# Linear attention and two feed-forward layers on one core: load order of the first pairs, order of the xh and xl pieces, place of the quotient steps and of layer two's weight conversions, queue of the x2 loads

## The chip, the cores and the metric

The kernel runs on one core of a Trainium2 chip. The metric is the device time of one execution in microseconds (us); lower is better. The engines are PE (matrix products), DVE (vector), ACT (scalar, with its activation functions), POOL (GpSimd) and SP (SyncE, which here issues almost all DMA transfers). Each engine works through its own instructions in order. A DMA issue stands in the stream of the engine that issues it, so an issue that waits holds up what is behind it.

## The reference

```python
# q, k, v: (4 batches, 8 heads, 576 tokens, 64); w_phi: (64, 128)
def phi(x):
    proj = np.einsum('bhsd,df->bhsf', x, w_phi)
    proj = proj - np.max(np.abs(proj), axis=-1, keepdims=True)
    return np.concatenate([np.exp(proj), np.exp(-proj)], axis=-1)
q_p, k_p = phi(q), phi(k)
kv = np.einsum('bhsf,bhsd->bhfd', k_p, v)
z = np.sum(k_p, axis=2)
num = np.einsum('bhsf,bhfd->bhsd', q_p, kv)
den = np.einsum('bhsf,bhf->bhs', q_p, z)[..., None] + 1e-06
x = (num / den).transpose(0, 2, 1, 3).reshape(2304, 512)
h = x @ w_in;   x2  = np.maximum(0.01 * h, h) @ w_out        # layer one: 512 -> 2048 -> 512
h = x2 @ w_in2; out = (h / (1 + np.exp(-h))) @ w_out2        # layer two: 512 -> 2048 -> 512
```

The weights of both layers reach the kernel as 64-bit words. The kernel turns them into 32-bit floats itself ("conversion").

## The kernel before

**Numbers in two pieces.** Most products are made from a high piece and a low piece of each operand: an ACT copy writes the rounded high piece, and DVE subtracts it from the value for the low one (`sub`, L262). Three products (high by high, high by low, low by high) replace one. Names ending in `h` and `l` are such pairs: `xh`/`xl`, `gh`/`gl`, `KVH`/`KVL`, `qh`/`ql`.

**Attention.** Work is in 16 pairs of heads, `(b, hp)`. Pairs 0 to 7 run first, in plain 32-bit (functions `f_...`): products of `k` (`f_pk` L418, `f_kt` L423/L429), of `q` (`f_pq` L453), a maximum over partitions on POOL (`f_pr` L475), exponentials on ACT (L301/L302, L493/L494), the sum over tokens (`kv_sign` L382/L387), its copy `KV` (`f_kc` L503), the quotient's products (`f_n` L516), their division (`f_nd` L532 to L534) and the writing of x (`f_fx`, through `put_x`). Pairs 8 to 15 run in high and low pieces (`s_...`): split of `k` and `q` (`s_split` L271, L279), the products of `k` (`s_pk`, L315 to L317), products of `q` (`s_pq` L347/L348, p copies L350, POOL maximum L352), `s_eq` (L362, L369, L370), the sum `s_kv` (L387, then `KVH` L400 on ACT and `KVL` on DVE), the numerator and denominator (`num_split`, L568, L571, L572), and `s_fin`. `num_split` sends the denominator through four DMAs: `e<-d`, then a reciprocal on DVE, `rec<-e`, `d<-rec`, all issued by SP. `s_fin` (fin0 and fin1 for the two halves of a pair) multiplies `x` by `d` (L588, DVE) and calls `put_x`, which for each token tile that the half touches makes `xh` (L408, ACT) and `xl` (DVE).

**Layer one.** 2304 tokens are five tiles of 462 or 460 (`tiles1`), and d_ff is 16 blocks of 128. A slot is one tile and one block: `h_mm` (12 products, L830), `h_g` (leaky relu into `g`, L836, ACT), `h_high` (`gh`, L841, ACT), `h_low` (`gl`, DVE), then `y_mm` (12 products, L861), one slot later in program order. A pair of the second half of the attention spans three slots, and the x of a tile is written about half a tile before the tile begins. After a tile, `y_out` stores it to `x2` in DRAM.

**Layer two.** `prep_x2` loads groups of 768 tokens from `x2` (`b1` L804, `b2` L805), forms four combinations of them on DVE (L808 to L811) and splits them. The layer is a seven-product scheme over 2 by 2 blocks. Its weights are prepared by `prep_w7` in units: load (L650), conversion on ACT (`narrow_act` L657, L658) and DVE (L664 to L670), sums (L717 to L720), split into `wst`, store to `w7s` (L713). `load_hl` loads them back as `ws` (L898); L942 and L1019 are the products. `raw` has 3 buffers (shared by weight words and `b1`/`b2`), `wst` 3 (shared with layer one's `wo` copies).

**What sets the order.** `ORDER`, `PLAN`, `SLOTS` and `EARLY` are hand-written times, sorted into one list `seq`; `run_att` takes steps from it and emits them. For engines in `pins` (PE, ACT, DVE), `in_order` notes the instructions of a step with its time, and `pin` chains those with a time under 150 in that order, without semaphores. All else is ordered by a scheduler that takes the program's order as priority and hoists what can run earlier. `behind(first, f)` emits `f` and ties each of its instructions behind the instruction in `first` of the same engine. `gate` is such a `first`: it holds layer two's conversions (`run_jobs`, `settle`) behind the split of pair 13's `k`. In `ORDER`, `flq` and `flv` are the loads of q/k and of v of pairs 0 to 7, all issued on SP; `va`, a pair's v, has 128 x 10 x 65 floats, 325 KB.

Of the kernel before, what the change touches and what calls it, by code (L numbers as in the profile page):

```python
# [18 lines left out]
    flq=(-0.1, 0.1, 0.4, 12.4, 23.9, 35.4, 46.9, 58.4),  # L19
    fpq0=(6.75, 10.01, 20.52, 27.8, 39.22, 50.72, 62.21, 73.71),  # L20
    fpq1=(7.22, 10.48, 20.99, 28.27, 39.69, 51.19, 62.68, 74.18),
    fpk=(4.47, 7.94, 21.45, 28.74, 40.16, 51.66, 63.15, 74.65),
# [12 lines left out]
    fqx0=(11.61, 19.16, 32.22, 44.23, 55.73, 67.22, 78.7, 89.4),  # L35
    flv=(0.0, 0.9, 22.9, 34.4, 45.9, 57.4, 68.9, 80.4),
    fqx1=(13.88, 22.28, 34.3, 45.8, 57.29, 68.79, 80.21, 91.65),
# [84 lines left out]
def tile_linear_attention_ffn_ffn(ctx: ExitStack, tc: tile.TileContext, q, k, v, w_phi, w_in1, w_out1, w_in2, w_out2, out):  # L122
# [48 lines left out]

    pins = {mybir.EngineType.PE: [], mybir.EngineType.Activation: [], mybir.EngineType.DVE: []}

# [9 lines left out]

    gate = {}

# [81 lines left out]
    def s_split(i):  # L267

        st = P[i]
        h, l = at([128, S0], F32R, "krh"), at([128, S0], F32R, "krl")  # L270
        a = nc.scalar.activation(h, st["kr"], AF.Copy)  # L271
        b = sub(l, st["kr"], h)
        if i == 13:
            gate.update({x.ins.engine: x.ins for x in (a, b)})
        st["krh"], st["krl"] = h, l
        qs = at([128, 2, S], F32R, "qs")
        for j in range(2):
            r, o = (slice(0, 64), slice(64, 128))[:: 1 - 2 * j]
            nc.scalar.activation(qs[r, j], st["qr"][r], AF.Copy)  # L279
            sub(qs[o, j], st["qr"][r], qs[r, j])  # L280
        st["qs"] = qs
        t = at([128, 128], F32R, "kth")
        nc.scalar.activation(t, st["kt"], AF.Copy)
        sub(t[64:128], st["kt"][64:128], t[64:128])
        st["kth"] = t
# [106 lines left out]
    def s_kv(i):  # L392
        st = P[i]
        for s in (1, 0):
            pv = kv_sign(i, s)
        h, l = st["KVH"], st["KVL"] = at([128, 2, 2, 2, D], F32R, "KVH"), at([128, 2, 2, 2, D], F32R, "KVL")
        for j in range(2):
            kv_, z_ = pv[:, :, j, 0:D], pv[:, :, j, D : D + 1].to_broadcast([128, 2, D])
            for slot, sr in ((j, kv_), (1 - j, z_)):
                nc.scalar.activation(h[:, j, :, slot, :], sr, AF.Copy)  # L400
                sub(l[:, j, :, slot, :], sr, h[:, j, :, slot, :])

    def put_x(i, rows, src, t0, n):

        b, hp = i // HP, i % HP
        for t, o, s0, n in segments(b * S + t0, n):
            xh, xl = x1_tile(t)
            nc.scalar.activation(xh[rows, hp, o : o + n], src[:, s0 : s0 + n], AF.Copy)  # L408
            sub(xl[rows, hp, o : o + n], src[:, s0 : s0 + n], xh[rows, hp, o : o + n])

# [219 lines left out]
    def run_att(until, tile_=None):  # L630
        while seq and (seq[-1][0] < until or (tile_ is not None and missing(tile_))):
# [8 lines left out]
            else:  # L640
                fns[n_](i)

# [151 lines left out]
    def prep_x2(u):  # L794
# [6 lines left out]
        for kk in range(2):  # L801
            b1 = wp.tile([128, 2, NB], F32, tag="raw", bufs=RAWB, name="b1")
            b2 = wp.tile([128, 2, NB], F32, tag="raw", bufs=RAWB, name="b2")
            nc.sync.dma_start(b1, x2[kk, :, a : a + 2 * NB].rearrange("p (j n) -> p j n", j=2))  # L804
            nc.sync.dma_start(b2, x2[kk + 2, :, a : a + 2 * NB].rearrange("p (j n) -> p j n", j=2))  # L805
            t1, t3 = (wp.tile([128, NB], F32, tag="t64", bufs=2, name="t1") for _ in range(2))
# [32 lines left out]
    def h_high(t, c):  # L839
        gh = G[t, c]["h"] = gp.tile([128, tiles1[t][1]], F32R, tag="gh", name="gh", bufs=2)  # L840
        nc.scalar.activation(gh, G[t, c]["g"], AF.Copy)  # L841

    def h_low(t, c):
        gl = G[t, c]["l"] = gp.tile([128, tiles1[t][1]], F32R, tag="gl", name="gl", bufs=2)
        sub(gl, G[t, c]["g"], G[t, c]["h"])

# [358 lines left out]
```

## Time and profile before

| what | value |
|---|---|
| median of 3 runs | 950.11 us (949.8 to 950.48) |
| profiled execution | 950.13 us |
| span of its instructions | 948.3 us, so 1.83 us lie around it |
| instructions | 15702 |

The span runs from the first to the last instruction that the profiler saw. What lies around it is in the time of an execution too. An engine that is idle costs time only where the work that ends last had to wait for it.

### The profile page before, as it was taken

Reading aid. Unit: us, or ns where it says so; the run is one execution under the profiler, and the core shown is the slowest. Engines: PE = TensorE matmul, PEld = TensorE weight load, DVE = VectorE, ACT = ScalarE, POOL = GpSimd, SP = SyncE. Lnnn points to the kernel's source line nnn. Section 1 sums busy time; section 2 is a strip of 40 time slices with the busy share of each in tenths; the row PEclk is TensorE's granted clock in tenths of the full one; section 3 lists DMA queues with packets and bytes.
Section 4 is the critical chain, followed back from the end, with each engine's and each line's share of the span. In section 5 each row is a group of like instructions: output and inputs, shape, how many; then the busy total and the mean of one; then the engine's idle time right before and its main releaser. Section 6 shows DMA issues by size and latency. Waiting matters only on the chain.

```text
span 948.3 us, 15702 instructions
## 1 busy us (share of the span) xinstructions
PE 937.1 (99%) x5430; PEld 883.5 (93%) x5430; DVE 649.2 (68%) x1280; ACT 596.3 (63%) x1224; POOL 70.6 (7%) x38
## 2 busy tenths in 40 slices
PE   8999999999999999999999999999999999999998
PEld 7999989999988989888888899999999999999998
DVE  6889999966676753478777667779653695534853
ACT  6888787877786765456655555566544565444553
POOL 3343000210112110000000000000000000000000
PEclk9999999999999999999999999999999999999999
DMA  9921474473343322599999988997898778986785
GB/s 339 373 76 59 135 253 152 175 228 105 119 143 110 118 101 66 196 354 366 366 335 343 408 309 285 337 335 277 273 299 278 238 241 264 305 272 222 249 265 171
DMA packets 102528, 226.14 MB, mean 238 GB/s; under 512 B 15024, under 2 KB 25264, under 8 KB 102448
## 3 DMA queue, kind: packets, MB, share of 16 engines
q1 hardware_dynamic: 102160, 224.86, 69.9%
q8 instruction: 44, 0.72, 0.3%
q14 instruction: 36, 0.29, 0.1%
q10 hardware_dynamic: 288, 0.26, 0.1%
HBM read 177.82 MB, written 47.22 MB: 237 GB/s over the span
## 4 chain that ended last, share of the span: by engine, by line
PE 84%; DMA 9%; ACT 4%; DVE 1%; SPq 1%; issue 1%; DVEq 0%; ACTq 0%
PE ps_y L1019 19%; PE ps_y L861 17%; PE ps_a L830 17%; PE ps_a L942 10%; PE ps_y L942 8%; PE ps_a L387 3%; DMA d<-rec 3%; DMA rec<-e 2%; PE ps_a L516 2%; PE ps_y L387 2%; DMA e<-d 1%; PE ps_y L516 1%; DMA w7s<-wst 1%; PE ps_a L568 1%; DMA ws<-w7s 1%
## 5 line engine op out<-in xcount | busy, mean ns | idle before, releaser
L830 PE MATMUL ps_a<-xh,wi 128*128 128x460 f32 (+1 forms) x640 | 196.3, 373 | 1.7 <-ACT g L836 1.6
L1019 PE MATMUL ps_y<-gt,ws 128*128 128x384 f32 x1008 | 177.5, 337 | 0.0
L1019 PEld LDWEIGHTS ps_y<-gt,ws 128*128 128x128 f32 x1008 | 176.4, 188 | 0.4 <-DMA ws<-w7s 0.4
L861 PE MATMUL ps_y<-gh,wo 128*128 128x460 f32 (+1 forms) x640 | 149.5, 372 | 1.1 <-ACT gh L841 1.1
L830 PEld LDWEIGHTS ps_a<-xh,wi 128*128 128x128 f32 x640 | 120.2, 188 | 16.3 <-ACT g L836 2.6
L861 PEld LDWEIGHTS ps_y<-gh,wo 128*128 128x128 f32 x640 | 119.2, 188 | 15.3 <-ACT gh L841 2.2
L830 PE MATMUL ps_a<-xl,wi 128*128 128x460 f32 (+1 forms) x320 | 118.8, 371 | 0.0
L942 PE MATMUL ps_a<-xs,ws 128*128 128x384 f32 x546 | 104.4, 338 | 0.5 <-DMA ws<-w7s 0.5
L942 PEld LDWEIGHTS ps_a<-xs,ws 128*128 128x128 f32 x546 | 96.7, 188 | 1.2 <-DMA ws<-w7s 0.8
L684 ACT ACTIVATE gt<-g 128x384 fp32r<-128x384 f32 x120 | 62.9, 525 | 53.3 <-PE ps_y L1019 51.8
L262 DVE TENSOR_TENSOR gt<-g,gt 128x384 fp32r<-128x384 f32 x120 | 66.3, 555 | 34.4 <-ACT gt L684 33.8
L942 PE MATMUL ps_y<-xs,ws 128*128 128x384 f32 x462 | 88.2, 338 | 0.4 <-DVE g L917 0.4
L942 PEld LDWEIGHTS ps_y<-xs,ws 128*128 128x128 f32 x462 | 81.7, 188 | 0.9 <-DVE g L917 0.7
L861 PE MATMUL ps_y<-gl,wo 128*128 128x460 f32 (+1 forms) x320 | 82.4, 373 | 0.0
L262 DVE TENSOR_TENSOR gl<-g,gh 128x460 fp32r<-128x460 f32 (+1 forms) x80 | 50.8, 635 | 25.5 <-ACT gh L841 16.0
L861 PEld LDWEIGHTS ps_y<-gl,wo 128*128 128x128 f32 x320 | 60.0, 188 | 6.9
L830 PEld LDWEIGHTS ps_a<-xl,wi 128*128 128x128 f32 x320 | 60.3, 188 | 6.0
L836 ACT ACTIVATE g<-ps_a 128x460 f32<-128x460 f32 (+1 forms) x80 | 44.0, 550 | 25.3 <-PE ps_a L830 24.6
L841 ACT ACTIVATE gh<-g 128x460 fp32r<-128x460 f32 (+1 forms) x80 | 46.7, 585 | 11.4 <-PE ps_y L861 10.2
L352 POOL PARTITION_ALL_REDUCE m<-p x16 | 35.3, 2208 | 236.1 <-ACT p L350 193.1
L387 PE MATMUL ps_a<-va,ke 128*128 128x128 f32 x384 | 46.9, 275 | 0.0
L934 ACT ACTIVATE g<-g 128x384 f32<-128x384 f32 x72 | 37.3, 520 | 14.8 <-DVE g L917 14.6
(168 smaller groups left out, 1501.0 us busy)
## 6 DMA issues: line engine op xcount, KB each, us to landing
ws<-w7s SPq DMA_DIRECT2D x336, 256.0 KB, 4.1
wo<-wos SPq DMA_DIRECT2D x64, 512.0 KB, 5.2
w7s<-wst SPq DMA_DIRECT2D x48, 512.0 KB, 6.2
raw<-in_moe_w_out_dram SPq DMA_DIRECT2D x32, 512.0 KB, 5.7
rawi<-in_moe_w_in_dram SPq DMA_DIRECT2D x16, 512.0 KB, 8.7
wos<-wo SPq DMA_DIRECT2D x16, 512.0 KB, 2.9
raw<-in_moe_w_in_dram SPq DMA_DIRECT2D x16, 512.0 KB, 6.7
va<-in_v_dram SPq DMA_DIRECT2D x16, 325.0 KB, 4.4
```

The costliest lines, as they stand in the source:

```text
L262: return nc.vector.tensor_tensor(out_, x, h.bitcast(F32), op=ALU.subtract)
L352: nc.gpsimd.partition_all_reduce(m, p, 128, bass_isa.ReduceOp.absmax)
L387: nc.tensor.matmul(pv[:, s, j], ke[:, g, s, :], vf[:, w : w + NKV], start=False, stop=(j == 1 and c == 3), skip_group_check=True)
L516: nc.tensor.matmul(pb[:, w : w + NNUM], e[:, s, cs], KV[:, s, j], start=(s == 0), stop=(s == 1))
L684: nc.scalar.activation(h, f, AF.Copy)
L830: nc.tensor.matmul(ph, a[:, kk, :], b_[:, kk, :], start=(m == 0), stop=(m == 3 * KD - 1))
L836: nc.scalar.activation(g, G[t, c]["ph"], AF.Prelu, alpha=0.01)
L841: nc.scalar.activation(gh, G[t, c]["g"], AF.Copy)
L861: nc.tensor.matmul(Y[t][d][:, 0:n], a[:, ds_], b_, start=(c == 0 and m == 0), stop=(c == NC - 1 and m == 1), skip_group_check=True)
L934: nc.scalar.activation(g[j], x, AF.Silu)
L942: nc.tensor.matmul(bank[b_], w[:, a, kk], x[:, c, kk], start=(first and m == 0), stop=(m == 5), skip_group_check=True)
L1019: nc.tensor.matmul(bank[b_][db], w[:, a, db], t[:, c], start=(first and p == 0 and m == 0), stop=(p == NP - 1 and m == 2), skip_group_chec ...
```

## The change

1. `ORDER`: the q products of pair 2 (`fpq0[2]`, `fpq1[2]`) move from 20.52/20.99 to 15.9/16.0, and the load of v of pair 0 (`flv[0]`) from 0.0 to 0.2, behind the q/k loads of pair 1.
2. `pins` also has SP, so DMA issues of steps that are emitted through `in_order` with a time under 150 (q/k/v loads, layer-one weight loads, stores of `wos`) are chained in the written order.
3. `put_x` makes all `xh` copies first, and then all `xl`.
4. `gate` is set by the last `KVH`/`KVL` of the last pair in place of the split of pair 13.
5. `low` holds the latest `gh` (ACT) and `gl` (DVE) emitted so far; fin0 and fin1 of pairs 8 to 15 are tied behind them.
6. The twelve loads of `x2` (384 KB each) are issued by GpSimd in place of SP.

```diff
-    fpq0=(6.75, 10.01, 20.52, 27.8, 39.22, 50.72, 62.21, 73.71),
-    fpq1=(7.22, 10.48, 20.99, 28.27, 39.69, 51.19, 62.68, 74.18),
+    fpq0=(6.75, 10.01, 15.9, 27.8, 39.22, 50.72, 62.21, 73.71),
+    fpq1=(7.22, 10.48, 16.0, 28.27, 39.69, 51.19, 62.68, 74.18),
...
-    flv=(0.0, 0.9, 22.9, 34.4, 45.9, 57.4, 68.9, 80.4),
+    flv=(0.2, 0.9, 22.9, 34.4, 45.9, 57.4, 68.9, 80.4),
...
-    pins = {mybir.EngineType.PE: [], mybir.EngineType.Activation: [], mybir.EngineType.DVE: []}
+    pins = {mybir.EngineType.PE: [], mybir.EngineType.Activation: [], mybir.EngineType.DVE: [], mybir.EngineType.SP: []}
...
-    gate = {}
+    gate, low = {}, {}
...
-        a = nc.scalar.activation(h, st["kr"], AF.Copy)
-        b = sub(l, st["kr"], h)
-        if i == 13:
-            gate.update({x.ins.engine: x.ins for x in (a, b)})
+        nc.scalar.activation(h, st["kr"], AF.Copy)
+        sub(l, st["kr"], h)
...
-                nc.scalar.activation(h[:, j, :, slot, :], sr, AF.Copy)
-                sub(l[:, j, :, slot, :], sr, h[:, j, :, slot, :])
+                ops = nc.scalar.activation(h[:, j, :, slot, :], sr, AF.Copy), sub(l[:, j, :, slot, :], sr, h[:, j, :, slot, :])
+        if i == B * HP - 1:
+            gate.update({x.ins.engine: x.ins for x in ops})
...
-        for t, o, s0, n in segments(b * S + t0, n):
-            xh, xl = x1_tile(t)
-            nc.scalar.activation(xh[rows, hp, o : o + n], src[:, s0 : s0 + n], AF.Copy)
-            sub(xl[rows, hp, o : o + n], src[:, s0 : s0 + n], xh[rows, hp, o : o + n])
+        parts = [(*[x[rows, hp, o : o + m] for x in x1_tile(t)], src[:, s0 : s0 + m]) for t, o, s0, m in segments(b * S + t0, n)]
+        for xh, xl, x in parts:
+            nc.scalar.activation(xh, x, AF.Copy)
+        for xh, xl, x in parts:
+            sub(xl, x, xh)
...
-                fns[n_](i)
+                behind(low if n_[:3] == "fin" else {}, fns[n_], i)
...
-            nc.sync.dma_start(b1, x2[kk, :, a : a + 2 * NB].rearrange("p (j n) -> p j n", j=2))
-            nc.sync.dma_start(b2, x2[kk + 2, :, a : a + 2 * NB].rearrange("p (j n) -> p j n", j=2))
+            nc.gpsimd.dma_start(b1, x2[kk, :, a : a + 2 * NB].rearrange("p (j n) -> p j n", j=2))
+            nc.gpsimd.dma_start(b2, x2[kk + 2, :, a : a + 2 * NB].rearrange("p (j n) -> p j n", j=2))
...
-        nc.scalar.activation(gh, G[t, c]["g"], AF.Copy)
+        low[mybir.EngineType.Activation] = nc.scalar.activation(gh, G[t, c]["g"], AF.Copy).ins
...
-        sub(gl, G[t, c]["g"], G[t, c]["h"])
+        low[mybir.EngineType.DVE] = sub(gl, G[t, c]["g"], G[t, c]["h"]).ins
```

## Rows read from the trace of the kernel before

**Rows 1.** The page: span, and busy us (share) of the engines.
```profile
span 948.3 us, 15702 instructions
...
PE 937.1 (99%) x5430; PEld 883.5 (93%) x5430; DVE 649.2 (68%) x1280; ACT 596.3 (63%) x1224; POOL 70.6 (7%) x38
```

**Rows 2.** Windows: busy us (x instructions) of each engine, granted clock, DMA share, GB/s.
```profile
0.00:20.00 20.00, 17.16 (x102) 14.52 (x103) 11.89 (x19) 13.41 (x30) 8.85 (x10) 1.00 0.91 327
...
260.00:280.00 20.00, 19.19 (x113) 17.55 (x112) 15.47 (x30) 15.26 (x35) 4.28 (x2) 1.00 0.51 165
...
380.00:400.00 20.00, 19.38 (x94) 17.16 (x93) 8.64 (x18) 9.53 (x19) 0.00 (x0) 1.00 0.51 165
...
640.00:660.00 20.00, 19.51 (x111) 19.05 (x110) 18.85 (x39) 12.20 (x27) 0.00 (x0) 1.00 0.72 260
760.00:780.00 20.00, 19.59 (x112) 19.27 (x111) 18.73 (x39) 12.82 (x28) 0.00 (x0) 1.00 0.77 239
```

**Rows 3.** Waits of PE in 219 to 366: sum in us, times, longest.
```profile
PE ps_a L830 <- ACT g L836: 1.6, 4, 0.8
PE ps_a L568 <- DVE KVL L262: 0.5, 1, 0.5
```

**Rows 4.** Chain that ended last, 219 to 262: start, us, what.
```profile
226.75 2.81 PE ps_a L830 x12
...
234.08 1.78 PE ps_a L387 x16
...
236.60 2.53 PE ps_a L830 x12
```

**Rows 5.** Timeline of the start: start, us, engine, line, out<-in, [idle before <-releaser].
```profile
8.99 1.10 PE L418 MATMUL ps_y<-wc,kr 128*128 128x256 f32 x4 [0.98 <-DMA kr<-in_k_dram]
...
10.19 1.94 DVE L483 TENSOR_TENSOR m<-p,m 128x512 f32<-128x512 f32 x1 [0.79 <-POOL m L475]
...
15.63 0.72 ACT L494 ACTIVATE qh<-m 128x640 f32<-128x640 f32 x1
...
16.15 0.68 DVE L483 TENSOR_TENSOR m<-p,m 128x512 f32<-128x512 f32 x1
...
16.59 0.60 ACT L503 ACTIVATE KV<-ps_y 128x512 f32<-128x512 f32 x1 [0.24 <-PE ps_y L387]
...
17.25 2.05 PE L516 MATMUL ps_y<-KV,qh 128*128 128x128 f32 x16 [0.69 <-ACT KV L503]
...
31.14 0.27 ACT L408 ACTIVATE xh<-ps_a 128x114 fp32r<-128x114 f32 x1 [1.37 <-DVE xl L262]
...
31.73 0.19 PEld L516 LDWEIGHTS ps_a<-KV,qh 128*128 128x128 f32 x1 [0.26 <-ACT p L464]
```

**Rows 6.** Timeline, attention beside layer one, and the first slots after it.
```profile
237.91 0.45 ACT L408 ACTIVATE xh<-x 128x288 fp32r<-128x288 f32 x1 [2.98 <-DVE x L588]
...
238.26 0.26 ACT L400 ACTIVATE KVH<-ps_a 128x128 fp32r<-128x128 f32 x1
...
268.73 0.66 ACT L657 ACTIVATE t<-raw 128x512 f32<-128x512 f32 x1
...
391.02 0.45 ACT L408 ACTIVATE xh<-x 128x288 fp32r<-128x288 f32 x1 [4.86 <-DVE x L588]
...
392.58 1.72 PE L861 MATMUL ps_y<-gh,wo 128*128 128x460 f32 x7 [0.62 <-ACT gh L841]
...
403.37 0.90 PE L861 MATMUL ps_y<-gh,wo 128*128 128x460 f32 x3 [0.51 <-ACT gh L841]
```

**Rows 7.** SP's queue in layer two: one row of its waits, then the timeline.
```profile
SPq L804 <- DVE t L810: 8.5, 1, 8.5
...
620.19 0.95 SPq L713 DMA_DIRECT2D w7s<-wst  x1
...
645.36 8.83 SPq L898 DMA_DIRECT2D ws<-w7s  x14
...
650.98 1.33 PE L942 MATMUL ps_a<-xs,ws 128*128 128x384 f32 x6 [0.49 <-DMA ws<-w7s]
```

## The prediction

> **What bounds the kernel now.** I read the page first. The span is 948.3 us and PE, the matmul engine, is busy for 937.1 of it [rows 1]; every window shows a granted clock of 1.00 [rows 2]. So nothing in this change can pay unless it closes a gap on PE: DVE, ACT and POOL are busy for 649.2, less and less again, and their idle time costs nothing by itself. The page leaves about 11 us of gaps. The windows say where some of them are: of 20 us PE misses 2.84 at the start, 0.81 in 260 to 280, 0.49 in 640 to 660, 0.41 in 760 to 780 [rows 2]. The waits of PE over 219 to 366 us, where full attention work runs beside layer one, name the releasers: four waits of L830 (layer one's first product) on `g` of L836, 1.6 us, longest 0.8, and one of L568 on `KVL`, 0.5 [rows 3].
>
> The idle column is not the whole price of a gap. In the chain that ended last, twelve L830 products after such a wait take 2.81 us and twelve with no wait ahead of them 2.53 [rows 4]. So a PE stall costs its idle time plus about 0.28 us. I use that below for every stall in the layer products.
>
> **The change, part by part.**
>
> *First pairs: load order and early products.* `flv[0]` goes behind both q/k loads, so pair 1's `kr` no longer queues behind pair 0's `va`, which is 325 KB; at the 327 GB/s that the first 20 us moved [rows 2] that is 1.0 us (estimate), as much as the 0.98 that L418 of pair 1 waits for `kr` [rows 5]. `va` itself lands about a load later and is read only after the exponentials of its pair. But the second gate of the prologue does not move with it: L516, the first quotient product, waits 0.69 for the copy `KV`, and that copy starts at 16.59 on ACT, which had been idle for only 0.24 after L494, an exponential of `q` that hangs on POOL and DVE, not on loads [rows 5]. So `KV` can come at most 0.24 us earlier. The rest of the saved 0.98 comes back as a hole ahead of L516, and `fpq0[2]`/`fpq1[2]` at 15.9/16.0 fill it with work that stood later; that pays only if what follows later does not wait anyway. It does: the conversions of layer-one weights on DVE and ACT. Their last visible gap is at 31.73, where the weight load of L516 waits 0.26 for an ACT copy (L464), itself behind `xh` (L408), which had stood 1.37 us waiting on DVE [rows 5].
>
> Pinning SP in the written order holds no load that is needed within about 10 us, and the `wos` stores that it also orders are read back only from the second token tile on; I cost it at nothing. If a pinned issue does stand in front of a needed load, the price is of the size of that 0.98.
>
> *`put_x`.* ACT makes both `xh` pieces, then DVE both `xl`. The second `xh` of the first pairs no longer waits for the first `xl` (the 1.37 of ACT). Same instruction count. On PE the visible part is the 0.26. Prologue together: 0.24 + 0.26 = 0.5. Bounds: 0 (all filled by the later DVE chain) and 0.98 + 0.69 = 1.7 (both waits vanish). I take 0.5, nearer to the lower end, since the 0.24 of ACT stands whatever the loads do.
>
> *Quotient steps held back (`low`).* Today the multiplication L588 of a finished quotient and its copy L408 stand ahead of other work on in-order engines, waiting for a DMA: ACT idles 2.98 us up to 237.91, and the `KVH` copies of the next pair (L400), which PE has had ready since 234.08 + 1.78 = 235.86 [rows 4], follow only at 238.26 [rows 6]. From these hang the POOL maximum, the next exponentials and then `g` of the third layer-one slot, which is what L830 waits for. Held behind the latest `gh` (ACT) and `gl` (DVE), `KVH` starts some 2 us earlier (238.26 - 235.86 = 2.4 at most); against that, the late `xh` (0.45) and its DVE steps of like size now fall into the busy stretch ahead of `g`. Net gain for `g` is about 2 - 0.45, minus what the ACT stretch takes back, around 1 us: more than the idle time of each stall (0.8 the longest). The quotient is itself read a token tile later, some 8 slots, so its delay is covered by tens of us; without that cover a late tile would cost one whole wait of this kind, 3 us. No DMA is issued by the held step. At the end of attention the same thing stands alone: `xh` of the last pair waits 4.86 us to 391.02, `g` and `gh` are queued behind it, and L861 stalls 0.62 to 392.58 [rows 6]. With `g` and `gh` first, that stall goes: 0.62 + 0.28 = 0.9.
>
> *Gate of layer two's weight conversions.* The first unit runs from 268.73 between the steps of pair 13: four ACT instructions of 0.66 (2.6 us) and more on DVE [rows 6]. This is the window with the least PE time of that stretch, and its stall is the 0.8 one [rows 3]. Now nothing starts before the last pair's `KVL`, some 100 us later. In 380 to 400 ACT and DVE are under half busy [rows 2]. Everything downstream has to fit in the end: the last store of converted weights is issued at 620.19 and the first loads of the bulk at 645.36 [rows 7], so about 20 us (estimate, after some 5 us to land) can be lost; I expect a delay of a few us, hidden by that slack.
>
> Five stalls in 219 to 366 fall under these two parts: idle 1.6 + 0.5 = 2.1, plus 5 x 0.28 = 1.4, so 3.5 us. Bounds: 0 if the order that replaces it is equally late, 3.5 above.
>
> *x2 loads on GpSimd's queue.* Twelve loads of 384 KB move. SP's queue stands 8.5 us on one of them (L804, for a buffer that DVE frees), and fourteen `ws` loads go out in 8.8 us from 645.36 behind it; PE waits for `ws` at 650.98, idle 0.49 [rows 7]. With L804 elsewhere the `ws` loads go as their buffers come free: 0.49 + 0.28 = 0.8 us. POOL has no other work after the attention, so nothing queues behind the waiting load there. What a GpSimd-issued load costs DVE, no row of before shows. The nearest is DVE's L483: 1.94 us while POOL computed, 0.68 without [rows 5], +1.26. DVE is most crowded in 640 to 660, 18.85 of 20 busy, so it can lose 1.15 there [rows 2]; at 1.26 for each of a group's four loads PE would wait 5.0 - 1.15 = 3.9 us longer. Bounds: 0 and 3.9. I take 0, as there POOL was computing on data and here it only starts transfers.
>
> The Trainium skill ("SBUF — State Buffer", section "Who interferes with whom") says that a DVE instruction with two SBUF inputs contends with a GpSimd instruction that reads SBUF, and that such instructions were not seen to slow the writing of DMA descriptors. Row and rule agree for L483, a subtraction of two SBUF operands; for the loads no run here shows it. By the rule the sum is 944.4, by the row up to 948.3.
>
> The Trainium skill ("DMA: Bandwidth & Descriptors", section "Issuing engines are not separate DMA queues") says that all issuers feed the same 16 engines, so another issuer saves only issue time. The row disagrees in part: the 8.5 us is a wait in SP's in-order stream, not transfer time, so by the row 0.8 is saved, by the rule nothing.
>
> *Sum.* 0.5 + 3.5 + 0.9 + 0.8 = 5.7 us. The profiled execution took 950.13 us (the median of the runs is 950.11): 950.13 - 5.7 = **944.4 us**. The stalls at 403 and 764 I leave as they are: they come from loads and stores crowding and from a DVE that is 18.73 of 20 us busy [rows 2, 6].
>
> **The rivals.**
>
> *A. The next thing is as late.* `g` comes earlier, yet L830 waits for something else in the same ACT queue. For it: what is put off lands in the same stretch of ACT. Against it: the stalls are short beside 2 us. Then only the 0.8 stall caused by the conversions (0.8 + 0.28) and the 650 stall (0.8) go: 950.13 - 1.9 = 948.2 us.
>
> *B. Slower: the held-back copies land ahead of `g`.* fin0 and fin1 each put one `xh` of 0.45 us into the ACT stretch that ends in a `g` for which PE already waits. If the head start of `KVH` does not reach `g`, because that stretch hangs on something else, each of the seven pairs beside layer one loses 0.9: 6.3 us, and the 3.5 are not won. 944.4 + 3.5 + 6.3 = 954.2 us. It decides per pair: the other parts gain 2.2, so the kernel is slower by 1.9 once a pair loses (2.2 + 1.9) / 7 = 0.6. For it: the waits on `g` show that this stretch has no slack. Against it: the head start, up to 2.4, is well over 0.9.
>
> *C. More goes.* The whole prologue bound (1.7 in place of 0.5) and the stalls at 403 (0.51 + 0.28) and 764 (0.41 + 0.28) too, as ACT and DVE queues are regrouped [rows 2, 6]: 944.4 - 1.2 - 0.8 - 0.7 = 941.7 us.
>
> *D. The transfers bound the 650 stall.* The `ws` loads also share engines with the x2 load (DMA share 0.72 in that window [rows 2]), so taking L804 out of the queue changes nothing: 944.4 + 0.8 = 945.2 us. The Trainium skill's section on issuing engines, named above, would have this.
>
> **How the numbers follow.** Likeliest, the sum: 0.56; D 0.11; A 0.17; C 0.07; B 0.09. The prediction is 944.4, its own range 942.5 to 947. A measurement of this kernel tells apart about 0.2%, 1.9 us: faster is below 948.2. The sum, C and D are faster; A lies on the border, half of it each way; B is slower. So faster 0.77, same 0.14, slower 0.09. The range reaches from C to beyond A and the 948.3 of GpSimd's upper bound: 941.5 to 950.0, with B and a little on the low side left out.
>
> **What would show it.** In the profile after: L418 of pair 1 near 8 us and a PE window 0 to 20 richer, but the first L516 still near 17; no L830 wait on `g` above 0.2 in 219 to 366; `KVH` ahead of `xh`; no L657 at 269 or anywhere before the last `KVL`; L861 at 391 without idle; no burst of `ws` loads and no wait at 650. Wrong would be: waits of L830 of the old size on another releaser (A), `xh` copies between `KVH` and `g` and longer waits on `g` (B), DVE instructions longer where GpSimd loads, PE waiting on `ws` for late converted weights, or a wait of layer one on `xh`.

## The result and the profile after

| kernel | time, median | runs |
|---|---|---|
| before | 949.95 us | 949.64 to 950.48, 4 runs |
| changed | 939.30 us | 938.98 to 939.63, 4 runs |

The ratio is 0.9887, with a 95% interval of 0.987 to 0.9904: faster by 10.65 us, where 5.7 were forecast. The time lies below the range of 941.5 to 950.0. The sign was right; the forecast gain was about half of the measured one. The profiled execution took 938.98 us.

The page of the changed kernel, span and engines, against [rows 1]:

```profile
span 937.2 us, 15718 instructions
...
PE 931.2 (99%) x5430; PEld 882.5 (94%) x5430; DVE 646.3 (69%) x1280; ACT 598.2 (64%) x1224; POOL 77.7 (8%) x50
```

The span is 11.1 us shorter. PE's own busy time fell by only 5.9 us, so half of what went was not listed as idle time before but lay inside PE's "busy" stretches.

Windows of the changed kernel, columns as in [rows 2]; the work in a window stands some us earlier than before:

```profile
0.00:20.00 20.00, 18.14 (x111) 14.82 (x112) 12.01 (x19) 13.42 (x30) 8.97 (x10) 1.00 0.80 267
...
260.00:280.00 20.00, 20.00 (x116) 18.49 (x115) 12.75 (x24) 16.25 (x34) 4.28 (x2) 1.00 0.41 133
...
380.00:400.00 20.00, 20.00 (x97) 18.02 (x96) 12.13 (x25) 10.87 (x21) 0.00 (x0) 1.00 0.77 283
...
640.00:660.00 20.00, 20.00 (x117) 20.00 (x116) 17.87 (x37) 10.03 (x20) 1.08 (x2) 1.00 0.93 312
760.00:780.00 20.00, 20.00 (x116) 20.00 (x115) 16.43 (x35) 10.38 (x21) 0.00 (x0) 1.00 0.87 279
```

From 260 on PE misses nothing in any of these windows. The granted clock (the 1.00 near the end of each row) is 1.00 in every window of both runs but the last, short one, where PE runs out of work (before 0.93 in 940 to 960, changed 0.92 in 920 to 940). No wait of PE after 24 us is left; the view of PE's waits (engine, line, what it waited for, sum, times, longest) has only these five rows:

```profile
PE ps_y L1052 <- DVE z L1050: 1.2, 1, 1.2
PE ps_y L429 <- ACT p L464: 0.8, 1, 0.8
PE ps_a L453 <- DMA qr<-in_q_dram: 0.3, 1, 0.3
PE ps_a L516 <- ACT KV L503: 0.2, 1, 0.2
PE ps_a L429 <- DMA kt<-in_k_dram: 0.2, 1, 0.2
```

The waits of [rows 3] have no successor. The waits on ACT and DVE that the prediction put behind them have shrunk too, over the whole run (before, `xh` waited 32.7 us for L588, and L588 34.8 us for `d`):

```profile
ACT xh L407 <- DVE x L588: 10.3, 13, 1.1
...
DVE x L588 <- DMA d<-rec: 2.2, 2, 1.8
```

The timeline of the start, against [rows 5]:

```profile
8.16 1.13 PE L418 MATMUL ps_y<-wc,kr 128*128 128x256 f32 x4
...
16.50 0.58 ACT L503 ACTIVATE KV<-ps_y 128x512 f32<-128x512 f32 x1
...
17.13 2.05 PE L516 MATMUL ps_a<-KV,qh 128*128 128x128 f32 x16 [0.20 <-ACT KV L503]
...
22.22 0.82 DVE L483 TENSOR_TENSOR m<-p,m 128x640 f32<-128x640 f32 x1
...
23.29 0.49 PE L429 MATMUL ps_y<-wc,kt 128*128 128x128 f32 x2 [0.78 <-ACT p L464]
```

L418 of pair 1 starts at 8.16 (before 8.99, with 0.98 idle), but L516 at 17.13 only 0.12 earlier, as ACT's `KV` moved by 0.09. Even that is chance: in six profiles with the changed start L516 comes between 17.13 and 17.74, and in six with the start of before between 17.05 and 17.59. L429 of pair 2 now waits 0.78 for an ACT copy.

The timeline of attention and of the slots after it, against [rows 6] (`KVH` is now L398, `xh` L407):

```profile
233.60 0.28 ACT L398 ACTIVATE KVH<-ps_a 128x128 fp32r<-128x128 f32 x1 [1.39 <-PE ps_a L385]
...
236.86 0.56 ACT L836 ACTIVATE g<-ps_a 128x462 f32<-128x462 f32 x1 [0.58 <-PE ps_a L830]
237.45 0.59 ACT L841 ACTIVATE gh<-g 128x462 fp32r<-128x462 f32 x1
...
238.63 0.45 DVE L588 TENSOR_TENSOR x<-x,d 128x288 f32<-128x288 f32 x1
...
239.12 0.45 ACT L407 ACTIVATE xh<-x 128x288 fp32r<-128x288 f32 x1 [1.07 <-DVE x L588]
...
360.15 0.66 ACT L657 ACTIVATE t<-raw 128x512 f32<-128x512 f32 x1
...
380.17 0.59 ACT L841 ACTIVATE gh<-g 128x460 fp32r<-128x460 f32 x1
...
384.77 0.43 ACT L407 ACTIVATE xh<-x 128x288 fp32r<-128x288 f32 x1
```

`KVH` waits for PE and for nothing else, `g` and `gh` follow from 236.86, and the multiplication and `xh` of the finished quotient stand behind them. The first conversion is at 360.15, where it had been at 268.73. At 384 the last `xh` is behind `gh`.

SP's and POOL's queues in layer two, against [rows 7]:

```profile
635.89 0.54 POOL L804 DMA_DIRECT2D b<-x  x1 [10.52 <-ACT xs L684]
...
613.45 45.42 SPq L898 DMA_DIRECT2D ws<-w7s  x44
```

The x2 load waits on POOL, 10.52 us for its buffer, and SP does not stand with it: up to 660 us, where this view ends, it issues 44 `ws` loads in one stream.

**Where the time went.** Four marks split a run: the first L830 product of slot 0, of slot 40 (just after attention's last products) and of slot 49, and the last L1019 product, all read from the timeline (a slot is twelve L830 products, counted in order). The table has the time up to slot 0 and then the three distances, in us, of one profiled execution each. The first column differs between executions of one kernel (83.92, 84.52 and 83.92 in three of the changed one), the others hardly.

| kernel | to slot 0 | 0 to 40 | 40 to 49 | 49 to last | profiled run |
|---|---|---|---|---|---|
| before | 85.19 | 298.72 | 44.49 | 516.10 | 950.13 |
| changed | 83.92 | 292.99 | 42.51 | 514.06 | 938.98 |
| gain | 1.27 | 5.73 | 1.98 | 2.04 | 11.15 |

The forecast by the same stretches was 0.5, 3.5, 0.9 and 0.8. The start of each slot, compared between the two runs, says where each gain arose:

| stretch | where the changed run gains, us |
|---|---|
| to slot 0 | 0.12 ahead of the first L516 product (chance, see above), 1.15 between it and slot 0 |
| 0 to 40 | five waits that the view of before names, near 226, 277, 304, 330 and 347: 0.76, 1.31, 0.76, 0.48, 0.94; near 221, 299 and 356, where it shows none: 0.19, 0.89, 0.32 |
| 40 to 49 | near 391, 403 and 424: 0.90, 0.81, 0.27 |
| 49 to last | near 650, 764 and 795: 0.89, 0.68, 0.34 |

The loss near 299 is in the run of before, but its view shows no idle time there:

```profile
298.92 0.29 PE L348 MATMUL ps_a<-qs,BDL 128*128 128x288 f32 x1
299.28 0.40 PE L347 MATMUL ps_a<-qs,WH 128*128 128x288 f32 x1
299.52 0.29 PE L348 MATMUL ps_a<-qs,BDL 128*128 128x288 f32 x1
299.90 0.48 PE L830 MATMUL ps_a<-xh,wi 128*128 128x462 f32 x1
```

These products start 0.36, 0.24 and 0.38 us apart, where the same ones at 287.50 start 0.13 apart. Each counts as busy for 0.29 us or more, so less than 0.1 us is left idle between two of them, and the delay hides in the busy time. What the table leaves of each stretch, 0.13 us at most, is spread.

### The profile page after: what moved, and what is told of

It is laid out like the page before. It is cut to its first block, busy times and chain, and to the rows that moved or that the text cites. A ratio compares the mean times of both kernels' runs of the same rounds, so it can differ in the third digit from the quotient of the medians.

```text
span 937.2 us, 15718 instructions
## 1 busy us (share of the span) xinstructions
PE 931.2 (99%) x5430; PEld 882.5 (94%) x5430; DVE 646.3 (69%) x1280; ACT 598.2 (64%) x1224; POOL 77.7 (8%) x50
## 4 chain that ended last, share of the span: by engine, by line
PE 97%; ACT 1%; DVE 1%; DMA 1%; POOL 0%; SPq 0%; issue 0%; DVEq 0%; ACTq 0%
PE ps_a L830 21%; PE ps_y L861 21%; PE ps_y L1019 19%; PE ps_a L942 10%; PE ps_y L942 9%; PE ps_a L385 5%; PE ps_a L568 3%; PE ps_a L516 2%; PE ps_y L385 1%; PE ps_y L516 1%; PE ps_a L380 1%; DMA qr<-in_q_dram 1%; PE ps_a L345 0%; PE ps_a L346 0%; PE ps_a L315 0%; PE ps_a L314 0%
## 5 line engine op out<-in xcount | busy, mean ns | idle before, releaser
L830 PE MATMUL ps_a<-xh,wi 128*128 128x460 f32 (+1 forms) x640 | 195.2, 372 | 0.0
L1019 PE MATMUL ps_y<-gt,ws 128*128 128x384 f32 x1008 | 177.2, 336 | 0.0
L1019 PEld LDWEIGHTS ps_y<-gt,ws 128*128 128x128 f32 x1008 | 176.5, 188 | 0.0
L861 PE MATMUL ps_y<-gh,wo 128*128 128x460 f32 (+1 forms) x640 | 148.5, 371 | 0.0
L830 PEld LDWEIGHTS ps_a<-xh,wi 128*128 128x128 f32 x640 | 120.3, 188 | 12.9
L861 PEld LDWEIGHTS ps_y<-gh,wo 128*128 128x128 f32 x640 | 119.5, 188 | 13.0
L830 PE MATMUL ps_a<-xl,wi 128*128 128x460 f32 (+1 forms) x320 | 118.7, 371 | 0.0
L262 DVE TENSOR_TENSOR gt<-g,gt 128x384 fp32r<-128x384 f32 x120 | 66.1, 555 | 32.2 <-ACT gt L684 31.5
L861 PE MATMUL ps_y<-gl,wo 128*128 128x460 f32 (+1 forms) x320 | 82.1, 373 | 0.0
L262 DVE TENSOR_TENSOR gl<-g,gh 128x460 fp32r<-128x460 f32 (+1 forms) x80 | 50.9, 636 | 34.4 <-ACT gh L841 20.0
L861 PEld LDWEIGHTS ps_y<-gl,wo 128*128 128x128 f32 x320 | 60.1, 188 | 6.9
L830 PEld LDWEIGHTS ps_a<-xl,wi 128*128 128x128 f32 x320 | 60.3, 188 | 6.0
```

Of the source, the lines that this page charges most:

```text
L262: return nc.vector.tensor_tensor(out_, x, h.bitcast(F32), op=ALU.subtract)
L830: nc.tensor.matmul(ph, a[:, kk, :], b_[:, kk, :], start=(m == 0), stop=(m == 3 * KD - 1))
L861: nc.tensor.matmul(Y[t][d][:, 0:n], a[:, ds_], b_, start=(c == 0 and m == 0), stop=(c == NC - 1 and m == 1), skip_group_check=True)
L1019: nc.tensor.matmul(bank[b_][db], w[:, a, db], t[:, c], start=(first and p == 0 and m == 0), stop=(p == NP - 1 and m == 2), skip_group_chec ...
```

## The experiments

The `u_` kernels undo one part of the change, the `o_` kernels make one part alone in the kernel before, the rest try something else. Medians are of 4 to 10 runs, the stretches of one profiled execution each; the control is the changed kernel, run three times.

| kernel | to slot 0 | 0 to 40 | 40 to 49 | 49 to last | median |
|---|---|---|---|---|---|
| changed (three profiles) | 83.92 to 84.52 | 292.99 to 293.00 | 42.51 | 514.06 | 939.22 to 939.40 |
| u_fin | 84.39 | 295.88 | 44.23 | 514.35 | 947.04 |
| u_gate | 84.39 | 294.33 | 42.51 | 514.06 | 940.47 |
| u_x2 | 84.36 | 292.99 | 42.51 | 518.69 | 944.59 |
| u_load (twice) | 84.20, 84.89 | 292.99 | 42.51 | 514.06, 514.48 | 939.76, 939.89 |
| u_putx | 84.98 | 293.07 | 42.51 | 514.06 | 940.17 |
| o_fin | 85.54 | 294.37 | 42.51 | 518.55 | 946.47 |
| o_nowait | 84.99 | 294.86 | 44.88 | 515.24 | 945.51 |
| o_gate | 85.39 | 296.33 | 45.93 | 515.51 | 948.17 |
| o_x2 | 85.44 | 299.76 | 44.85 | 514.24 | 948.41 |
| o_fin_x2 | 85.12 | 294.39 | 42.51 | 514.06 | 941.41 |
| o_putx | 84.85 | 298.16 | 44.91 | 516.21 | 948.85 |
| v_pc | 85.40 | 293.00 | 42.51 | 514.06 | 940.54 |
| v_q | 85.83 | 292.99 | 42.51 | 514.06 | 940.95 |
| v_q_u | 86.36 | 293.17 | 42.51 | 514.06 | 941.51 |

**u_fin: the fin steps not held.**

```diff
-                behind(low if n_[:3] == "fin" else {}, fns[n_], i)
+                fns[n_](i)
```

> The changed kernel with fin0/fin1 no longer tied behind gh and gl. Theory (each part removes its own stalls): the stalls on g near 226, 304 and 330, the one on KVL near 346 and the one on gh near 391 of the kernel before come back, 0.56 + 0.56 + 0.5 + 0.8 + 0.9 = 3.3 us, so about 942.6 against 939.3 of the changed kernel; up to 943.6 if the smaller ones at 221, 299, 352 and 355 come with them. Rival (the later conversions freed ACT and DVE, the fin steps did not matter): at most 940.3, stalls only at 391.

Measured: 947.04, 0.9967 of before (0.9951 to 0.9983): 7.7 us above the changed kernel, where the theory had 3.3. The profiled execution, 944.32, was the fastest of six (up to 947.71), so the slower ones lose up to 3.4 us more, which no trace shows. In its profile 2.89 us come back before slot 40 and 1.72 between 40 and 49. The timeline shows the old picture:

```profile
339.92 0.46 DVE L588 TENSOR_TENSOR x<-x,d 128x288 f32<-128x288 f32 x1 [2.40 <-DMA d<-rec]
...
340.42 0.44 ACT L407 ACTIVATE xh<-x 128x288 fp32r<-128x288 f32 x1 [3.69 <-DVE x L588]
...
343.60 0.37 PE L568 MATMUL ps_a<-qh,KVH 128*128 128x288 f32 x1 [0.53 <-DVE KVL L262]
...
389.14 1.92 PE L861 MATMUL ps_y<-gh,wo 128*128 128x460 f32 x8 [0.68 <-ACT gh L841]
```

DVE stands 2.40 us on `d<-rec`, then ACT on L588, then PE on `KVL`; at 389 `gh` is late in the same way. The stalls at 304 and 330 did not come back, though, which the theory had counted.

**u_gate: conversions released by pair 13 again.**

```diff
-        nc.scalar.activation(h, st["kr"], AF.Copy)
-        sub(l, st["kr"], h)
+        a = nc.scalar.activation(h, st["kr"], AF.Copy)
+        b = sub(l, st["kr"], h)
+        if i == 13:
+            gate.update({x.ins.engine: x.ins for x in (a, b)})
...
-        if i == B * HP - 1:
-            gate.update({x.ins.engine: x.ins for x in ops})
```

> The changed kernel with the conversions of layer two released by pair 13's split again. Theory: only the stall near 277 and some of the two near 299 come back, 1.1 to 1.8 us, so 940.4 to 941.1. Second theory: the stalls near 403 and 424, too, depend on when the conversions' stores run; then 941.3 to 942.0. Rival (holding back the fin steps is enough): 939.3 to 939.6.

Measured: 940.47, about 1.2 us above the changed kernel. Stretch 0 to 40 is 1.34 longer; the waits of PE in it are one row:

```profile
PE ps_a L830 <- ACT g L836: 0.8, 1, 0.8
```

The first theory holds; 403 and 424 are untouched by the gate.

**u_x2: x2 loads on SP again.**

```diff
-            nc.gpsimd.dma_start(b1, x2[kk, :, a : a + 2 * NB].rearrange("p (j n) -> p j n", j=2))
-            nc.gpsimd.dma_start(b2, x2[kk + 2, :, a : a + 2 * NB].rearrange("p (j n) -> p j n", j=2))
+            nc.sync.dma_start(b1, x2[kk, :, a : a + 2 * NB].rearrange("p (j n) -> p j n", j=2))
+            nc.sync.dma_start(b2, x2[kk + 2, :, a : a + 2 * NB].rearrange("p (j n) -> p j n", j=2))
```

> The changed kernel with the x2 loads on SP again. Theory: SP waits some 8 us on one x2 load, the ws loads behind it come late, and the stall near 640 (650 before) is back, 0.8 us: 940.1. If the stalls of 764 and 795 belong to it as well, 941.1. Rival (a load's issuer is of no account, the transfers are shared): 939.3.

Measured: 944.59, and the last stretch 518.69 - 514.06 = 4.63 us longer: all numbers were too small, the mechanism was as described. SP's wait on the x2 load, PE's wait, and the chain behind it (start, us, what):

```profile
SPq L804 <- DVE t L810: 10.2, 1, 10.2
...
PE ps_a L942 <- DMA ws<-w7s: 2.1, 1, 2.1
PE ps_y L942 <- DVE g L917: 0.4, 1, 0.4
```

```profile
639.31 4.38 DMA ws<-w7s
...
643.82 1.29 PE ps_a L942 x6
645.12 5.06 PE ps_y L1019 x20
```

SP stands 10.2 us, not 8.5. PE then idles 2.14, and twenty L1019 products take 5.06 us where 276 in one piece took 48.30 in the chain of before (0.175 each, so 3.5): another 1.6 us are lost with no idle time shown: from the third of them to the thirteenth they start 0.32 us apart, and the `ws` loads land one by one, some 0.67 us apart, so each pair seems to wait for its own weights. The 764 stall is back as well (0.4 on `g` of L917, at 759).

**u_load and u_load_again: old load order, SP unpinned.**

```diff
-    fpq0=(6.75, 10.01, 15.9, 27.8, 39.22, 50.72, 62.21, 73.71),
-    fpq1=(7.22, 10.48, 16.0, 28.27, 39.69, 51.19, 62.68, 74.18),
+    fpq0=(6.75, 10.01, 20.52, 27.8, 39.22, 50.72, 62.21, 73.71),
+    fpq1=(7.22, 10.48, 20.99, 28.27, 39.69, 51.19, 62.68, 74.18),
...
-    flv=(0.2, 0.9, 22.9, 34.4, 45.9, 57.4, 68.9, 80.4),
+    flv=(0.0, 0.9, 22.9, 34.4, 45.9, 57.4, 68.9, 80.4),
...
-    pins = {mybir.EngineType.PE: [], mybir.EngineType.Activation: [], mybir.EngineType.DVE: [], mybir.EngineType.SP: []}
+    pins = {mybir.EngineType.PE: [], mybir.EngineType.Activation: [], mybir.EngineType.DVE: []}
```

> The changed kernel with the three old times in ORDER and SP unpinned; put_x stays. Theory: pair 1's kr waits behind va again and the first KV and the first products of pair 1's quotient slip; of the 1.3 us that the prologue gained 0.3 to 0.9 go: 939.6 to 940.2. Rival (prologue gain is all put_x's): 939.3. Other rival (pinning SP is what matters, loads of weights no longer run ahead of kr and va): all 1.3, 940.6.

> The changed kernel with the old three times in ORDER and SP unpinned, now timed on one chip with its control. Theory (put_x alone carries the prologue's gain): within 0.3 us of the control. Rival (the prediction: half of the prologue's gain comes from kr and KV): 0.3 to 0.6 slower.

> The changed kernel as control for the run below: 939.2 to 939.6.

Measured: 939.76, and on one chip with its control 939.89 (938.88 to 940.77) against 939.40 (938.84 to 940.28). The runs overlap, so the times settle nothing. The traces do, for the stretch from the first L516 product to slot 0, which is the same to 0.01 us in all profiles of one kind:

| start of the kernel | profiles | first L516 to slot 0 |
|---|---|---|
| as before | before, o_fin, o_gate, o_x2, o_fin_x2, o_nowait | 67.94 to 67.95 |
| changed, old `put_x` | u_putx | 67.94 |
| old load order, new `put_x` | o_putx, u_load, u_load_again | 67.30 to 67.31 |
| changed | changed (three), u_fin, u_gate, u_x2 | 66.78 to 66.79 |

So parts 1 and 2 (load order, early q products, SP pinned) gain nothing alone and 0.52 us with the new `put_x`. That is the size of the first theory but not its place: the gain lies behind L516, and no gain of `kr` or `KV` ahead of it shows in the profiles. Which of the three edits gives it was not separated.

**u_putx and o_putx: the order of the pieces.** u_putx puts the old loop back; o_putx makes the new one alone.

```diff
-        for xh, xl, x in parts:
-            nc.scalar.activation(xh, x, AF.Copy)
-        for xh, xl, x in parts:
-            sub(xl, x, xh)
+        for t, o, s0, n in segments(b * S + t0, n):
+            xh, xl = x1_tile(t)
+            nc.scalar.activation(xh[rows, hp, o : o + n], src[:, s0 : s0 + n], AF.Copy)
+            sub(xl[rows, hp, o : o + n], src[:, s0 : s0 + n], xh[rows, hp, o : o + n])
```

> The changed kernel with put_x as before: each xl right behind its xh. Theory after the first set (putting the load order back cost nothing, 0.2 us less if anything): the 1.3 us that the prologue gained are put_x's, so 940.6. Rival (the prediction: 0.26 of it): 939.6. Rival (it is the early q products and the loads together, and either can stand in): 939.3.

> The kernel before with only put_x's new order. Theory: slot 0 of layer one comes 0.7 to 1.1 us earlier than in the kernel before (85.2 to 85.5 in its profiles), 84.4 to 84.7; the time 949.1, unless the wait for ws eats it. Rival (prediction): 0.26 us, slot 0 at 85.0 or later.

> The changed kernel itself, as the control on the chip of this set: 939.3 to 939.8. Its profile gives the start of the kernel on the same chip as the one below without put_x's new order; the start differs a little from chip to chip (slot 0 of layer one at 83.9 in one profile of it, at 84.4 in three of the first set).

Measured: u_putx 940.17 (940.11 to 940.54) against 939.22 (938.87 to 939.59) of the control on the same chip, 0.95 us, with no overlap. o_putx 0.9984 of before (0.9973 to 0.9996), slot 0 at 84.85, between what its theory and its rival had. By the table above the new order gains 0.64 us alone, and 1.16 in the changed kernel, since without it the 0.52 of parts 1 and 2 is lost too.

**o_fin: the hold alone.** The `behind(low, ...)` line and the two lines that fill `low`, in the kernel before.

```diff
-                fns[n_](i)
+                behind(low if n_[:3] == "fin" else {}, fns[n_], i)
...
-        nc.scalar.activation(gh, G[t, c]["g"], AF.Copy)
+        low[mybir.EngineType.Activation] = nc.scalar.activation(gh, G[t, c]["g"], AF.Copy).ins
...
-        sub(gl, G[t, c]["g"], G[t, c]["h"])
+        low[mybir.EngineType.DVE] = sub(gl, G[t, c]["g"], G[t, c]["h"]).ins
```

> The kernel before with only the fin steps tied behind gh and gl. Theory: what undoing it cost, 4.7 us, is gained, and the stalls at 304 and 330 go too, since they were absent in both kernels with one of the two holds: 950.0 - 4.7 - 1.0 = 944.3; the one at 277 and those at 650 and 764 stay. Rival (it pays only together with the later conversions): gain under 3, over 947.

Measured: 0.9964 of before (0.9951 to 0.9977), 946.47. Up to slot 49 it gains 298.72 - 294.37 + 44.49 - 42.51 = 6.3 us, more than forecast: the stalls at 304, 330, 403 and 424 go too. Then it gives back 518.55 - 516.10 = 2.45, and the view of waits names the place:

```profile
SPq L804 <- DVE t L810: 10.2, 1, 10.2
...
PE ps_a L942 <- DMA ws<-w7s: 2.0, 1, 2.0
```

**o_fin_x2: the hold and the x2 loads on GpSimd, nothing else.** The diff of o_fin, and that of u_x2 the other way round.

> The kernel before with the fin steps held back and the x2 loads on GpSimd, nothing else. Theory (the fin steps alone gained 6.4 us by the end of layer one and gave 3 back at the wait for ws, because SP stood longer on an x2 load; GpSimd's queue takes that away): 950.0 - 6.4 - 1.8 = 941.8, no wait of PE for ws. Rival (late ws has another cause, such as weights converted too late): over 944 with the stall near 644 still there.

Measured: 941.41 (941.2 to 941.65), 0.9906 of before (0.9888 to 0.9923). Two of the six parts give 950.13 - 941.56 = 8.6 of the 11.15 us between the profiled runs. The last stretch is 514.06, as in the changed kernel, and PE does not wait for `ws`.

**o_x2: the x2 loads alone.** The diff of u_x2, the other way round.

> The kernel before with only the x2 loads on GpSimd. Theory: the stalls of 650, 764 and 795 go, 0.75 + 0.7 + 0.3 = 1.75 us: 948.2. It gives less than undoing it costs the changed kernel (4.6), because there the layer-two weights come later and the same wait in SP's queue hits more. Rival (764 belongs to the DVE's load and not to the queue): 949.2. Rival (the loads' issuer is of no account): 949.95.

Measured: 0.9982 of before (0.9972 to 0.9992), 948.41, with runs from 946.99 to 949.87. The last stretch falls by 1.86, as expected, the stall at 764 included. The profiled run lost 1.0 between slots 0 and 40, at waits on `KVL` and `g` like those of [rows 3].

**o_gate: the later conversions alone.** The diff of u_gate, the other way round.

> The kernel before with only the gate of layer two's conversions moved to the last pair. Theory: the stall near 277 (1.0) and those at 299, 304 and 330 (1.9), absent in the kernel with this hold and without the other, go: 2.9 us by slot 36 of layer one; then more is lost at the wait for ws near 648 as layer one ends sooner, up to 2. So 947.2 to 949. Rival (prediction: 1.08 and nothing else): 948.9 with the stalls at 304 and 330 in place.

Measured: 0.9971 of before (0.9959 to 0.9982), 948.17, runs from 945.79 to 949.85. Stretch 0 to 40 is 2.39 shorter: the stalls at 277, 304 and 330 are gone. But 40 to 49 is 1.44 longer; that the conversions meet the fin steps there, which still stand in the queues, is likely, not shown. So the stalls at 304 and 330 are gone with either hold; that is why, in the profiles up to slot 40, undoing one part at a time brings back less than making it alone gains. With the fin steps held, the gate is worth the stall at 277 and no more: 4.35 (o_fin) and 1.34 (u_gate) make 5.69 of the 5.73.

**o_nowait: the work of before, without the wait.** L588 multiplies `x` by itself, so the output is not the quotient; the DMA chain still runs.

```diff
-            nc.vector.tensor_mul(x, x, st["r", a])
+            nc.vector.tensor_mul(x, x, x)
```

> The kernel before with L588 multiplying x by itself and not by the reciprocal: the step has the same operation and size but does not wait for the DMA chain, which is still issued (the output is not the quotient). No hold, no other change. Theory (what holding the fin steps gained is the wait for the DMA at the head of DVE's and ACT's queues, not the work of the steps): by slot 40 of layer one as early as with the hold, 379.5 to 380 (before 383.9), and by slot 49 422 (428.4); then part is lost at the wait for ws, as there: 946 to 947. Rival (the work of the steps crowds g): slot 40 at 383 or later, 949.5.

Measured: 945.51, 0.9959 of before (0.9944 to 0.9975). Slot 40 starts at 379.85, with the hold at 379.91; the stretch before it is 3.86 shorter than before, with the hold 4.35. So the work of the steps costs at most the 0.49 us between the two, and the rest is the wait. Its timeline:

```profile
228.38 0.46 DVE L588 TENSOR_TENSOR x<-x 128x288 f32<-128x288 f32 x1 [0.31 <-ACT x L572]
...
230.16 0.44 ACT L408 ACTIVATE xh<-x 128x288 fp32r<-128x288 f32 x1
...
234.81 0.28 ACT L400 ACTIVATE KVH<-ps_a 128x128 fp32r<-128x128 f32 x1 [2.02 <-PE ps_a L387]
```

The same `xh` that came at 237.91 is done at 230.6, and `KVH` waits only for PE. But the order is not that of before: with no DMA to wait for, the scheduler puts these steps earlier, this `xh` ahead of `gh`, where it had stood behind it. So the run shows that the steps' work does little harm, even ahead of `gh`, when it waits for nothing. It does not show the wait taken away with every step in its old place. Slot 49 came at 424.72 and not 422: stretch 40 to 49 is 44.88, 2.37 over that with the hold, and 1.5 of it is one wait of L861 on `gh` that ends at 420.21. The stall at 403 is gone here as with the hold. For the rest of that stretch the theory fails: it depends on the order at the end of attention too, not on this wait alone.

**v_pc: earlier copies of pair 2's q products.**

```diff
-    fpc0=(7.05, 11.04, 20.89, 28.89, 40.9, 52.39, 63.89, 75.35),
+    fpc0=(7.05, 11.04, 17.0, 28.89, 40.9, 52.39, 63.89, 75.35),
```

> The changed kernel with the first copies of pair 2's q products (fpc0[2]) written at 17.0 in place of 20.89, so that the bank they hold comes free before L429 of pair 2 asks for it (a wait of 0.78 at 23.3). Theory (that wait is on the path of the prologue): slot 0 is 0.5 to 1.0 earlier, 938.5. Rival (DVE's conversions set the pace by then): unchanged, 939.3.

Measured: 940.54, 1.2 us slower than the changed kernel. The wait of L429 is gone, but POOL's next maximum now starts earlier and meets DVE's subtraction:

```profile
22.57 2.06 POOL L475 PARTITION_ALL_REDUCE m<-p  x1 [1.58 <-ACT qh L494]
22.74 1.79 DVE L483 TENSOR_TENSOR m<-p,m 128x640 f32<-128x640 f32 x1
...
24.57 0.38 ACT L464 ACTIVATE p<-ps_a 128x256 f32<-128x256 f32 x1 [1.08 <-DVE m L483]
```

L483 takes 1.79 us where it took 0.82 in the changed kernel, and ACT waits 1.08 us behind it.

**v_q and v_q_u: q of pair 0 first.** v_q_u has the old load order besides.

```diff
+        if i == 0:
+            nc.sync.dma_start(st["qr"], q[i])
...
-        nc.sync.dma_start(st["qr"], q[i])
+        if i:
+            nc.sync.dma_start(st["qr"], q[i])
...
-    fpq0=(6.75, 10.01, 15.9, 27.8, 39.22, 50.72, 62.21, 73.71),
-    fpq1=(7.22, 10.48, 16.0, 28.27, 39.69, 51.19, 62.68, 74.18),
+    fpq0=(4.0, 10.01, 15.9, 27.8, 39.22, 50.72, 62.21, 73.71),
+    fpq1=(4.1, 10.48, 16.0, 28.27, 39.69, 51.19, 62.68, 74.18),
```

> The changed kernel with pair 0's q loaded first and its two q products ahead of its k products, so that POOL's maximum starts some 2 to 3 us earlier (8.4 in the changed kernel). Theory (the prologue hangs on POOL's first maximum through the exponentials of q and KV): slot 0 0.5 to 1 earlier, 938.5. Rival (k comes later and DVE's and ACT's k steps then set KV): unchanged or up to 0.5 slower.

> The same with the old three times in ORDER and SP unpinned. Theory (load order and early q products of pair 2 gain nothing once put_x is there): as the run above to 0.3 us. Rival (pinning matters once q comes first): 0.5 or more slower than it.

Measured: 940.95 and 941.51, slower than the changed kernel by 1.6 and 2.2. POOL starts at 7.01 instead of 8.44, but the k side comes late (lines of v_q; behind L418 they stand three later than in the changed kernel):

```profile
7.01 1.95 POOL L478 PARTITION_ALL_REDUCE m<-p  x1 [5.69 <-ACT p L467]
...
9.31 0.69 DVE L293 TENSOR_REDUCE km<-ps_y 128x4 f32<-128x512 f32 x1 [4.08 <-PE ps_y L421]
...
18.43 0.58 ACT L506 ACTIVATE KV<-ps_y 128x512 f32<-128x512 f32 x1
```

DVE's first k step is at 9.31 (5.19 before that edit), and `KV` at 18.43 (16.50). The theory falls: earlier q costs more on the k side than it gains. v_q_u is 0.56 slower than v_q, as its rival had it. No kernel tried beats the changed one.

## Why the prediction was right in kind and short by half

**What came was the likeliest case and most of rival C.** None of the rivals A, B and D happened. PE has no wait on `g` left (against A), `xh` stands behind `g` and `gh` (against B), and the 650 stall is gone and comes back with the loads on SP (against D). The stalls at 403 and 764 went as well, which the sum left standing and C, at a chance of 0.07, let go; about half of what C added to the prologue came too. Two steps of the prediction failed, and the prologue's accounts were off.

- *"Five stalls in 219 to 366 fall under these two parts", 3.5 us.* Measured 5.73 in slots 0 to 40; this is the mis-sized term. The five came to 4.25 and not 3.5, and three more places, near 221, 299 and 356, gave 1.40. There the view names no wait, as the products only follow each other more slowly. The step that failed is to take the waits that the view names for all that is lost. The mechanism, in-order engines standing on a DMA, held: with the fin steps behind `gh` and `gl` alone 4.35 us are gained, and in o_nowait, where the same steps wait for nothing, 3.86. The gate's own stall was sized nearly right, 0.8 + 0.28 = 1.08 against 1.34 in u_gate.
- *"The stalls at 403 and 764 I leave as they are."* They went, with two smaller ones at 424 and 795 that the sum does not name: 0.81 + 0.27 and 0.68 + 0.34, together 2.1 us. The stall at 403 was put down to loads and stores crowding, but o_fin, which moves only the fin steps, removes it and the one at 424. By which link is not settled, since o_nowait has a stall of its own at 420. The one at 764 was put down to a crowded DVE, but o_x2 removes it with the same 39 DVE instructions in 760 to 780 (17.82 us busy, before 18.73).
- *End of attention, 0.9 us, and x2 loads, 0.8 us.* The two stalls that these terms price were sized right: 0.90 near 391 and 0.89 near 650. What these stretches gained beyond that are the four stalls just named. The price of the old queue is not fixed: SP's wait of 8.5 us costs PE 0.5 idle, one of 10.2 costs 2.0 to 2.1 and, in u_x2, 1.6 more in slowed products. With the fin steps held the wait is the longer one, so putting the loads on GpSimd is worth 1.86 us alone and 4.63 in the changed kernel.
- *Prologue, 0.24 + 0.26 = 0.5 us.* The time up to L516 shows no gain beyond its spread, so the 0.24 for `KV` is not seen; L516's 0.12 in one pair of profiles is luck. Behind L516 1.16 us were gained. `put_x`, put at 0.26, is worth 0.64 alone, and the early q products with the loads 0.52 on top of it.
- *GpSimd's price, 0.* Right: a load takes POOL 0.54 us to issue, and the subtractions of DVE (L262, 128x384, two SBUF operands) that ran during such an issue took 549 to 553 ns, as the rest of them (medians 552 to 558). The Trainium skill ("SBUF — State Buffer", section "Who interferes with whom") would have it so, and for L483 against POOL's maximum v_pc shows the contention it describes: 1.79 us against 0.82.
- *Rival D* drew on the Trainium skill ("DMA: Bandwidth & Descriptors", section "Issuing engines are not separate DMA queues"): another issuer saves only issue time. u_x2 disagrees by 4.6 us: what another issuer saved here is the wait of a blocked load, which held fourteen others.

The chances were also added up wrongly: the sum, C, D and half of A make 0.83 for a faster kernel, not 0.77. What was missing is a bound from above. Twelve products take 2.53 us unhindered [rows 4]; that unit could have been held against the spacing of all products of the stretch and not against five waits. How near 5.7 it would have come from the run of before alone is not worked out here.

## What to carry to other kernels

On in-order engines a step that waits for a DMA should be emitted behind the work that PE waits for, even if it is ready first in the program's order: here that was worth 6 us up to slot 49, and the same steps did little harm where they waited for nothing. Do not price such an edit by the waits that a view names for the bound engine; compare the spacing of its instructions in the stretch with their spacing where nothing is late. A load that must wait for a buffer belongs on a queue where nothing urgent stands behind it, and what that is worth can grow when the stages before it get faster (here from 1.9 to 4.6 us).

## What the runs showed of the hardware beyond that

- The kernel before varies from run to run (946.77 to 955.0 over the chips used) much more than the changed one (938.84 to 940.28) or o_fin_x2 (941.2 to 941.65). The kernels with the fin steps unheld or the x2 loads on SP vary by 2.1 to 4.1 us (u_fin, u_x2, o_fin, o_nowait, o_x2, o_gate, o_putx). That they depend on when single DMAs land, and the others do not, is argued, not shown.
- The same kernel's first layer-one product came at 83.92 in two executions and at 84.52 in another; the later distances agree to 0.01 us. The difference arises in the first loads: in six profiles with the same start L418's first eight products ended at 6.0 us (twice) or at 7.3 to 7.4 (four times).
- A subtraction of DVE took 1.79 us instead of 0.82 when POOL's maximum overlapped it; in v_pc, where POOL came earlier, the kernel was slower by 1.2 us.
